# The output product of attention with tokens as the stationary side, and layer norm 2 token block by token block, in an attention-and-mixer kernel

## The chip, the cores and the metric

The kernel runs on one core of a Trainium2 chip. A core has a matrix engine (TensorE, here PE, with PEld for its loads of the stationary operand), VectorE (DVE), ScalarE (ACT), GpSimd (POOL) and SyncE (SP), each with its own instruction stream, and DMA queues between the chip's memory and the on-chip memory. Matmul results go to banks of 128 x 512 floats, from which VectorE and ScalarE read. The metric is the device time of one execution in microseconds (us).

## What is computed

One layer in float32: layer norm, attention in four segments of 512 tokens with a memory carried from one segment to the next, an output product with a residual, a second layer norm, and an MLP with a residual.

```
x = A_x                                      # 1 x 2048 x 1024, 32 heads of 32
o = attention(layernorm(x))                  # 4 segments of 512, causal in each, gated with the memory
h = x + o @ wo                               # wo 1024 x 1024
y = layernorm(h)
h2 = h + gelu(y @ w1 + b1) @ w2 + b2         # w1 1024 x 3584, w2 3584 x 1024
```

## The kernel before

Every product is made of three matmuls, since each operand is split into a high and a low part (`split`, L86): high times high, high times low, low times high (`mm3`, L113). A split is a cast on ScalarE (L90) and a subtraction on VectorE or GpSimd (L91). The moving side of a matmul has 512 columns, the stationary side 128.

The program runs over two halves of 1024 tokens, each of two segments (`sl` 0 and 1) of 512 tokens, and each segment of four token blocks of 128. A half has these stages:

1. attention over groups of four heads (eight groups a segment). Its result `ot` (128 features x 512 tokens) is written to `o_dram`, and `load_o` (L622) reads it back, split into `oh`, `ol`;
2. the output product of segment 0, `wo_seg` (L635), interleaved with the end of attention: 1.3 steps of attention for each of the first 14 steps, then 0.7 (`RA`, `RH`, `RS`). Loads of segment 1's outputs are spread among the steps from step 28 (`PD`) on, every third step (`PS`);
3. the output product of segment 1, again `wo_seg`, interleaved with layer norm 2 of segment 0 (`ln2`, one step of it for two of the product). Here TensorE keeps program order (`in_order(PE)`), the other engines are ordered by the scheduler;
4. `Mixer.lead`: the MLP's first products (`cps`, 24 matmuls per block of features: `c1` and `c2`) on segment 0's tokens, all engines in program order. Beside it, 0.4 side steps per step, run layer norm 2 of segment 1 and `fold`, which transposes the normed tokens and makes the sums and differences of the two segments' tokens that the later products read;
5. 14 times `Mixer.pair`, and in half 1 the second MLP product.

`wo_seg` takes `wo` in eight blocks of 128 columns (`load_block`, L289). A block is the stationary side, the 512 tokens move, so the result `pwo` has features on the partitions. `finish` copies it with ScalarE to `at` (L657); its `fold` transposes `at` in four pieces with TensorE into `pn` (L662), and VectorE adds the four pieces to four token blocks `ht` (L666), which hold `x` at first. A token block has its sum when all eight column blocks are through. `pwo`, `pn` and layer norm's transposes `pt` all turn through the same three banks (`ps_dense`).

Layer norm 2 takes statistics with VectorE (L121, L125) and the scale and offset with GpSimd (L128 to L134, `nb`), norms with ScalarE (L163); `residual` adds `b2` (`hb`, L686) and stores it. `ln_transpose` then turns the block with TensorE (`pt`, L142), casts it on ScalarE (`zh`, L144) and subtracts on VectorE (`zl`, L146). In the lead, the product's first part is copied by ScalarE (`p`, L831) and stored by a DMA that ScalarE issues; the GELU is L779; the weights `wx` are cast on ScalarE (L806) and subtracted on VectorE (L812).

Of the kernel before, what the change touches and what calls it, by code (L numbers as in the profile page):

```python
# [9 lines left out]
F32 = mybir.dt.float32  # L10
# [6 lines left out]
P = 128  # L17
# [8 lines left out]
NG = 8  # L26
HT = 1024
NT = HT // P
RA, RH, RS, PD, PS = 1.3, 14, 0.7, 28, 3
# [13 lines left out]
def build(tc, x, wq, wk, wv, wo, beta, w1, b1, w2, b2, out):  # L43
# [253 lines left out]
    def attention(half, first):  # L297
# [254 lines left out]
        def av_out(st):  # L552
# [82 lines left out]
    def wo_seg(half, sl, hts, tp, extra, evac):  # L635
        blk, wts = {}, {}

        def prods(c, gs):
            for k in (c, c + 1):
                if k < DC and k not in wts:  # L640
                    wts[k] = load_block(wp, wo, k * P, 3, "scalar", "gpsimd" if k % 2 else "vector")
            if c not in blk:
                blk[c] = wts[c] + (ps_dense("pwo"),)
            wh, wl, ps = blk[c]
            oh, ol = acts["o", sl]
            for g in gs:
                mm3(ps, wh[:, g, :], wl[:, g, :], oh[:, g, :], ol[:, g, :], g == 0, g == NG - 1)
                next(extra, None)
                if g == 3:
# [5 lines left out]
        def finish(c):
            at = tp.tile([P, 512], F32, tag="tmp", name="at", bufs=5)
            nc.scalar.copy(at, blk[c][2])  # L657

            def fold():
                pn = ps_dense("pn")  # L660
                for t in range(4):
                    op = nc.tensor.transpose(pn[:, t * P:(t + 1) * P], at[:, t * P:(t + 1) * P], ident)  # L662
                    if t == 0:
                        tc.add_manual_dep(op.ins, acts["mm"].ins.name, NOSYNC, reason="program order")
                for t in range(4):
                    nc.vector.tensor_tensor(hts[t][:, c * P:(c + 1) * P], pn[:, t * P:(t + 1) * P],  # L666
                                            hts[t][:, c * P:(c + 1) * P], op=ALU.add)
            evac.append(fold)

        yield from prods(0, range(NG - 1))  # L670
        yield from prods(1, range(NG - 1))
        if sl == 0:
            load_o(half, sl, NG - 1, tp)
        for c in range(DC):
            yield from prods(c, range(NG - 1, NG) if c < 2 else range(NG))
            finish(c)
# [20 lines left out]
    def ln2_combined(half, hts, zx, pp):  # L697
        for _ in range(3):
            yield
        zh, zl = seg_tiles(1, "z")  # L700
        ts = {n: [zx.tile([P, 4, 512], F32R, tag=f"t{x_}{n}", name=f"t{x_}{n}") for x_ in "hl"] for n in (1, 2, 3)}
# [49 lines left out]
        yield from ln_tiles(lnp, hts, None, None, True, 2, act=True, fold=fold, aside=residual(half, 1, hts, pp))  # L751
# [14 lines left out]
    class Mixer:  # L766
# [22 lines left out]
        def begin(self):  # L789
# [27 lines left out]
            lower(-1)  # L817
            self.early = load, upper, lower, left

        def lead(self):  # L820
# [19 lines left out]
            load(1)  # L840
# [448 lines left out]
```

## Time and profile before

| what | value |
|---|---|
| time, median of 3 runs | 2388.07 us (2385.95 to 2391.18) |
| the profiled execution, its own time | 2383.26 us |
| its span, first to last instruction | 2381.4 us |
| granted TensorE clock, mean | 0.995 |
| segment 0's output product, half 0 and 1 | 71.26 and 69.67 us |
| segment 1's output product | 56.94 and 57.90 us |
| `Mixer.lead` | 88.41 and 88.15 us |

The stage times are from one stage's first matmul to the next stage's, in the profiled execution. A row of the profile names a line of the kernel, an engine, an operation and the tiles, out<-in; in a timeline the number behind `<-` in brackets is the time that the engine stood idle before and what released it. A row of the busy time by stage gives, for each engine, busy us and instructions, then the granted clock (1.00 is full), the DMA engines' busy share and GB/s. A row of the waits gives who waited for whom, us in total, how many times, and the longest.

### The profile page before, as it was taken

How to read it: one execution, taken by the hardware profiler on the slowest of the kernel's cores; microseconds unless marked ns; L12 is line 12 of the kernel's file. 1: busy time of each engine (PE TensorE's matmuls, PEld its weight loads, DVE VectorE, ACT ScalarE, POOL GpSimd, SP SyncE). 2: the span in 40 equal slices, each digit the busy share in tenths (PEclk: the TensorE clock that was granted, in tenths of full speed). 3: DMA queues.
4: the chain of work that ended last, by engine and by line, in shares of the span. 5: the costliest groups of instructions: out<-in, count | busy, mean ns of one | idle time of the engine just before them, and what ended most of it. 6: DMA issues, size and time to landing. Idle time of an engine off the chain costs nothing.

```text
span 2381.4 us, 35726 instructions
## 1 busy us (share of the span) xinstructions
PE 2305.1 (97%) x11873; PEld 1905.9 (80%) x11873; DVE 1571.3 (66%) x3420; ACT 1244.0 (52%) x2587; POOL 1083.3 (45%) x1045
## 2 busy tenths in 40 slices
PE   7999999999999999999999999999999999999999
PEld 5888888877777887888888877787888788888887
DVE  5777777775466555777777776456566676566653
ACT  5676676775364344677777776354334223222321
POOL 4444444444255443455555544235444464246430
PEclk9999999999999999999999999999999999999999
DMA  5333333333466554433333334456557976476762
GB/s 164 98 89 89 83 84 85 89 106 121 144 197 204 181 168 136 124 84 88 84 84 87 81 100 125 148 168 208 164 172 224 347 261 223 154 243 229 251 220 96
DMA packets 348306, 357.49 MB, mean 150 GB/s; under 512 B 26302, under 2 KB 251610, under 8 KB 348122
## 3 DMA queue, kind: packets, MB, share of 16 engines
q1 hardware_dynamic: 284954, 318.50, 44.8%
q10 hardware_dynamic: 63168, 36.71, 5.2%
q8 instruction: 94, 1.54, 0.3%
q14 instruction: 90, 0.74, 0.1%
HBM read 227.64 MB, written 77.14 MB: 128 GB/s over the span
## 4 chain that ended last, share of the span: by engine, by line
PE 72%; DVE 7%; ACT 7%; DMA 4%; POOL 3%; issue 3%; SPq 1%; ACTq 0%; DVEq 0%; POOLq 0%
PE po L1137 21%; PE bps L762 8%; PE dps L762 5%; PE ppt L525 5%; PE po L545 5%; PE pqk L493 3%; PE kps L114 2%; PE kps L116 2%; PE kps L115 2%; PE pwo L114 2%; PE pwo L115 2%; PE pwo L116 2%; PE vps L115 2%; PE vps L114 2%; PE vps L116 2%
## 5 line engine op out<-in xcount | busy, mean ns | idle before, releaser
L509 POOL TENSOR_SCALAR pr<-pr,nm,gate 128x128 f32<-128x128 f32 (+3 forms) x512 | 323.8, 643 | 409.0 <-DVE nm L506 316.3
L502 ACT ACTIVATE pr<-pr,mx 128x256 f32<-128x256 f32 (+3 forms) x512 | 287.8, 563 | 174.8 <-DVE mx L494 170.4
L494 DVE CUSTOM_DVE_ANT_0 pr<-pqk,mask 128x256 f32<-128x256 f32 (+3 forms) x512 | 243.5, 483 | 38.2 <-PE pqk L493 35.5
L532 DVE TENSOR_TENSOR ptl<-ppt,pth 128x512 fp32r<-128x512 f32 (+1 forms) x384 | 227.3, 597 | 59.2 <-ACT pth L527 56.9
L525 PE MATMUL ppt<-ident,pr 128*128 128x128 f32 x1280 | 222.7, 277 | 1.9 <-DVE ptl L532 1.7
L527 ACT CAST pth<-ppt 128x512 fp32r<-128x512 f32 (+1 forms) x384 | 194.2, 518 | 51.3 <-PE ppt L525 46.0
L1147 DVE TENSOR_TENSOR c<-c,po 128x512 f32<-128x512 f32 x160 | 105.3, 683 | 150.4 <-PE po L1137 150.3
L91 POOL TENSOR_TENSOR wl<-wr,wh 128x1024 fp32r<-128x1024 f32 x61 | 145.9, 2392 | 115.1 <-ACT wh L90 57.2
L525 PEld LDWEIGHTS ppt<-ident,pr 128*128 128x128 f32 x1280 | 164.1, 140 | 32.2 <-DVE ptl L532 3.6
L493 PE MATMUL pqk<-ks,qs 96*128 96x256 f32 (+3 forms) x512 | 163.1, 319 | 1.5 <-DVE mx L494 1.5
L545 PE MATMUL po<-ptl,vs 128*64 128x512 f32 (+3 forms) x512 | 154.3, 311 | 5.5 <-DVE ptl L532 5.2
L545 PE MATMUL po<-pth,vs 128*64 128x512 f32 (+3 forms) x512 | 155.7, 326 | 1.3 <-ACT pth L527 1.1
L1137 PE MATMUL po<-w2h,zh 128*128 128x512 f32 x378 | 120.7, 389 | 0.0
L493 PEld LDWEIGHTS pqk<-ks,qs 96*128 96x128 f32 x512 | 96.2, 188 | 26.6 <-DVE mx L494 6.5
L506 DVE RECIPROCAL nm<-mx 128x2 f32<-128x2 f32 x256 | 42.2, 165 | 112.4 <-ACT pr L502 111.9
L1007 POOL TENSOR_TENSOR w2r<-w2r 128x512 f32<-128x512 f32 x54 | 84.3, 1574 | 59.4 <-DMA w2r<-in_B_w 54.6
L114 PE MATMUL kps<-yh,wh 128*128 128x512 f32 x256 | 108.5, 424 | 0.8 <-ACT yh L144 0.8
L114 PE MATMUL vps<-yh,wh 128*128 128x512 f32 x256 | 108.8, 425 | 0.2 <-ACT omt L475 0.2
L114 PE MATMUL qps<-yh,wh 128*128 128x512 f32 x256 | 107.0, 418 | 0.0
L114 PE MATMUL pwo<-oh,wh 128*128 128x512 f32 x256 | 105.7, 415 | 0.7 <-ACT oh L90 0.7
L1137 PE MATMUL po<-w2h,hl 128*128 128x512 f32 x322 | 102.9, 389 | 1.3 <-DVE c L1147 1.3
L116 PE MATMUL pwo<-oh,wl 128*128 128x512 f32 x256 | 102.0, 399 | 0.0
(244 smaller groups left out, 6751.5 us busy)
## 6 DMA issues: line engine op xcount, KB each, us to landing
hr<-h_dram SPq DMA_DIRECT2D x112, 448.0 KB, 4.7
w2r<-in_B_w SPq DMA_DIRECT2D x122, 256.0 KB, 4.4
r<-in_B_w SPq DMA_DIRECT2D x56, 512.0 KB, 4.7
h_dram<-ht ACTq DMA_DIRECT2D x84, 256.0 KB, 3.4
ks<-kh SPq DMA_DIRECT2D x256, 64.0 KB, 2.0
qs<-qh SPq DMA_DIRECT2D x256, 64.0 KB, 2.0
wr<-in_A_wo SPq DMA_DIRECT2D x32, 512.0 KB, 4.4
wx<-in_B_w SPq DMA_DIRECT2D x56, 256.0 KB, 3.8
```

The lines of the kernel that those rows point to most:

```text
L114: nc.tensor.matmul(ps, ah, bh, start=first, stop=False)
L116: acts["mm"] = nc.tensor.matmul(ps, al, bh, start=False, stop=last)
L493: nc.tensor.matmul(pqk[:, :n], u["qs"][j][:, i * P:(i + 1) * P], u["ks"][j][:, 0:n], start=True, stop=True)
L494: nc.vector.tensor_tensor_reduce(out=st["pr"][:, offs[i]:offs[i] + n], in0=pqk[:, :n], in1=mask[:, 512 - n:512], op0=ALU.add, op1=ALU.min, ...
L502: nc.scalar.activation(pi, pi, AF.Exp, bias=mx[:, i:i + 1], scale=-1.0, accum_out=mx[:, 4 + i:5 + i])
L509: nc.gpsimd.tensor_scalar(pi, pi, nm[:, 4 + k:5 + k], gate[:, 1, 4 * g + j:4 * g + j + 1], op0=ALU.mult, op1=ALU.mult)
L525: nc.tensor.transpose(ppt[:, o:o + P], pr[:, offs[i] + jk * P:offs[i] + (jk + 1) * P], ident)
L527: nc.scalar.copy(pth[:, base:base + w], ppt[:, :w])
L532: nc.vector.tensor_tensor(o, x0, x1, op=ALU.subtract)
L545: nc.tensor.matmul(po[:, P * jk:], v, st[part][:, koff[jk]:koff[jk] + w], start=(jk, part) == (0, "pth"), stop=(jk, part) == (2, "ptl"))
L762: nc.tensor.matmul(ps, x_[:, c, :], y_[:, c, :], start=first and c == 0 and n == 0, stop=last and c == 3 and n == 2, skip_group_check=True)
L1137: nc.tensor.matmul(ps, x_[:, k], y_[k], start=opens and k == 0 and i == 0, stop=closes and k == self.KP - 1 and i == 2, skip_group_check=True)
```

## The change

Now 128 tokens of the attention output are the stationary side, and `wo` moves in halves of 512 columns. A result `pwo` has tokens on the partitions and is added to `ht` straight from its bank, by one VectorE instruction (L670 of the changed kernel). The copies `at`, the transposes `pn` and the 128-column adds are gone. The number of product matmuls is the same: two halves `n` by four token blocks `t`, eight groups and three matmuls in each, 192 a segment. `wo` is still loaded in 512 KB pieces, eight a segment, now as 256 rows by 512 columns.

- `wo_first` (segment 0) takes the blocks (n, t) in the order (0,0), (0,1), both without the last group of heads at first, then (0,2), (0,3), (1,0) to (1,3). Two of its weight quarters lie in tiles of a new pool `zt`.
- `wo_second` (segment 1) takes (0,0), (0,1), (1,0), (1,1), (0,2), (1,2), (0,3), (1,3). When both halves of a token block are done, `ready` runs layer norm 2's statistics, residual and norm for it (`ln2_token`). For block 3 they stay in the lead, as do all four `fold`s, which there have no norm between them.
- The last group of attention outputs is split straight from `ot`, without the way through `o_dram`. `PD` is 16 in place of 28. `load(1)` of the mixer's weights is issued in `begin`, within the second product, not at the lead's start.

```diff
-RA, RH, RS, PD, PS = 1.3, 14, 0.7, 28, 3
+RA, RH, RS, PD, PS = 1.3, 14, 0.7, 16, 3
...
-                nc.sync.dma_start(o_dram[u["s"]][u["g"]], ot)
+                if u["g"] < NG - 1:
+                    nc.sync.dma_start(o_dram[u["s"]][u["g"]], ot)
+                else:
+                    oh, ol = o_tiles(half, u["s"] % 2)
+                    split(None, ot, oh[:, NG - 1, :], ol[:, NG - 1, :], hi_eng="scalar", lo_eng="vector")
...
+    def wo_raw(n, k):
+        wr = wp.tile([P, DC, P], F32, tag="wr", name="wr", bufs=2).rearrange("p a b -> p (a b)").rearrange("p (c n) -> p c n", c=2)
+        nc.sync.dma_start(wr, wo[k * 256:(k + 1) * 256, n * 512:(n + 1) * 512].rearrange("(c p) n -> p c n", p=P))
+        return wr
+    def wo_halves(wr, k, home):
+        h, l = home
+        split(None, wr, h, l, "scalar", "gpsimd" if k % 2 else "vector")
+        return h, l
+    def wo_home():
+        return [wp.tile([P, DC, P], F32R, tag=t, name=t, bufs=3).rearrange("p a b -> p (a b)")
+                .rearrange("p (c n) -> p c n", c=2) for t in ("wh", "wl")]
+    def wo_block(half, sl, hts, blk, wts, extra, n, t, gs=range(NG), after=None):
+        if (n, t) not in blk:
+            blk[n, t] = ps_dense("pwo")
+        ps, cols = blk[n, t], slice(t * P, (t + 1) * P)
+        oh, ol = o_tiles(half, sl)
+        for g in gs:
+            wh, wl = wts[n, g // 2]
+            mm3(ps, oh[:, g, cols], ol[:, g, cols], wh[:, g % 2], wl[:, g % 2], g == 0, g == NG - 1)
+            next(extra, None)
+            if after:
+                after(g)
+            if g == NG - 1:
+                o = hts[t][:, n * 512:(n + 1) * 512]
+                nc.vector.tensor_tensor(o, blk.pop((n, t)), o, op=ALU.add)
+            yield
+    def wo_first(half, hts, extra):
+        wts, blk, raws = {}, {}, {}
+        more = [zx_tile(x_, 3) for x_ in "hl"]
+        for k in range(4):
+            wts[0, k] = wo_halves(wo_raw(0, k), k, wo_home() if k < 3 else [x_[:, 0:2] for x_ in more])
+        block = partial(wo_block, half, 0, hts, blk, wts, extra)
+        def turn(g):
+            if g == 0:
+                raws[1] = wo_raw(1, 1)
+            if g % 2 and g < NG - 1:
+                k = g // 2 + 1
+                if k not in raws:
+                    raws[k] = wo_raw(1, k)
+                wts[1, k] = wo_halves(raws[k], k, wo_home())
+        for t in (0, 1):
+            yield from block(0, t, range(NG - 1))
+        for t in (0, 1):
+            yield from block(0, t, range(NG - 1, NG))
+        wts[1, 0] = wo_halves(wo_raw(1, 0), 0, [x_[:, 2:4] for x_ in more])
+        yield from block(0, 2)
+        yield from block(0, 3, after=turn)
+        yield from block(1, 0)
+        acts["raw"] = [wo_raw(0, k) for k in (0, 1)]
+        for t in range(1, 4):
+            yield from block(1, t)
         for _ in extra:
             pass
+    def wo_second(half, hts, ready):
+        wts, blk = {}, {}
+        zxs = {m: [zx_tile(x_, m) for x_ in "hl"] for m in (1, 2, 3)}
+        def weights(n, k):
+            m = 2 * n + k // 2 + 1
+            home = [z[:, 2 * (k % 2):2 * (k % 2) + 2] for z in zxs[m]] if m < 4 else wo_home()
+            wr = acts["raw"][k] if n == 0 and k < 2 else wo_raw(n, k)
+            wts[n, k] = wo_halves(wr, k, home)
+        for k in range(4):
+            weights(0, k)
+        def blocks():
+            block = partial(wo_block, half, 1, hts, blk, wts, iter(()))
+            for n, t in ((0, 0), (0, 1), (1, 0), (1, 1), (0, 2), (1, 2), (0, 3), (1, 3)):
+                for g, _ in enumerate(block(n, t)):
+                    if n == 0 and t < 2 and g % 4 == 1:
+                        weights(1, 2 * t + g // 4)
+                    yield
+                if n == 1:
+                    ready(t)
+        return blocks()
...
-        yield from ln_tiles(lnp, hts, None, None, True, 2, act=True, fold=fold, aside=residual(half, 1, hts, pp))
+        for t in range(4):
+            yield from fold(hts[t], t)
+    def ln2_token(half, hts, pp, t):
+        m, r = ln_scale(lnp, hts[t], True)
+        nb = ln_offset(lnp, m, r)
+        residual(half, 1, hts, pp)(t)
+        yield
+        nc.scalar.activation(hts[t], hts[t], AF.Identity, bias=nb, scale=r)
+        yield
 
...
             lower(-1)
+            load(1)
             self.early = load, upper, lower, left
...
-            load(1)
             for j in (0, 1):
...
+        mixer = Mixer(half, mq)
+        last_token = []
+
+        def ready(t):
+            steps = ln2_token(half, hts1, pp, t)
+            if t < 3:
+                for _ in steps:
+                    pass
+            else:
+                last_token.append(steps)
+
+        second = wo_second(half, hts1, ready)
+        load_x(half, 1, hts1)
         nc.sync.dma_start(acts["b2"], bass.AP(tensor=b2.tensor, offset=b2.offset, ap=[[0, P], [1, D]]))
-        load_x(half, 1, hts1)
-        mixer = Mixer(half, mq)
         with in_order(mybir.EngineType.PE):
-            interleave(hooked(wo_seg(half, 1, hts1, pp, iter(()), evac), lambda k: mixer.begin(), 57, 1),
+            interleave(hooked(second, lambda k: mixer.begin(), 57, 1),
                        ln2(half, 0, hts, pp), 0.5)
         acts.pop("last")
 
         def ln2_last():
             yield
-            yield
-            for e in evac:
-                e()
-            yield from ln2_combined(half, hts1, zx, pp)
+            next(last_token[0])
+            side = ln2_combined(half, hts1)
+            for n, _ in enumerate(side):
+                if n == 1:
+                    next(last_token[0])
+                yield
```

Of the program's instructions 128 go on TensorE (11875 to 11747), 96 on VectorE (3398 to 3302), 32 on ScalarE (2217 to 2185); GpSimd keeps its 1050, SyncE has 1490 in place of 1498.

First, TensorE in half 0, where layer norm 2 of segment 0 begins. Before, `ht_6844` is the first token block, and its transposes stand behind those of the last two column blocks:

```order
L114 MATMUL pwo<-oh_7317,wh 128x512
L115 MATMUL pwo<-ol_7318,wh 128x512
L116 MATMUL pwo<-oh_7317,wl 128x512
L662 MATMUL pn<-ident,at 128x128 [waits Activation_49]
L662 MATMUL pn<-ident,at 128x128 x3
L662 MATMUL pn<-ident,at 128x128 [waits Activation_49]
L662 MATMUL pn<-ident,at 128x128 x3
L142 MATMUL pt<-ident,ht_6844 128x128 [waits DVE_49]
L142 MATMUL pt<-ident,ht_6844 128x128 x3
```

After, the first token block is `ht_6847`, and `zh_7497`, `wh` and their low parts hold quarters of `wo`:

```order
L114 MATMUL pwo<-zh_7497,oh_7177 128x512
L115 MATMUL pwo<-zl_7498,oh_7177 128x512
L116 MATMUL pwo<-zh_7497,ol_7178 128x512
L142 MATMUL pt<-ident,ht_6847 128x128 [waits DVE_49]
L142 MATMUL pt<-ident,ht_6847 128x128 x3
L114 MATMUL pwo<-wh,oh_7177 128x512 [waits Activation_49]
L115 MATMUL pwo<-wl,oh_7177 128x512 [waits DVE_49]
L116 MATMUL pwo<-wh,ol_7178 128x512
```

The transposes of layer norm 2 follow the product directly, and the product's next matmuls wait for casts and subtractions of weights that stand on ScalarE and VectorE.

Second, VectorE in the second output product of half 0. Before (`zl_7624` is layer norm 2 of segment 0, `ht_7560` to `ht_7563` the token blocks of segment 1):

```order
L666 TENSOR_TENSOR ht_7560<-pn,ht_7560 128x128 [waits PE_49]
L666 TENSOR_TENSOR ht_7561<-pn,ht_7561 128x128
L666 TENSOR_TENSOR ht_7562<-pn,ht_7562 128x128
L666 TENSOR_TENSOR ht_7563<-pn,ht_7563 128x128
L146 TENSOR_TENSOR zl_7624<-pt,zh_7623 128x4x128 [waits Activation_49]
L91 TENSOR_TENSOR wl<-wr,wh 128x1024 [waits DMAHW4_49,PE_49,Activation_49]
L146 TENSOR_TENSOR zl_7624<-pt,zh_7623 128x4x128 [waits Activation_49]
```

After (`ht_7488` and `ht_7489` are the first two token blocks of segment 1, `ht_6850` the last of segment 0):

```order
L91 TENSOR_TENSOR wl<-wr,wh 128x1024 [waits DMAHW0_49,Activation_49]
L670 TENSOR_TENSOR ht_7489<-pwo,ht_7489 128x512 [waits PE_49]
L872 TENSOR_TENSOR wl<-wx,wh 128x512 [waits DMAHW3_49,Activation_49]
L121 BN_STATS st<-ht_7489 128x6 [waits DVE_49]
L121 BN_STATS st<-ht_6850 128x6 x2
L146 TENSOR_TENSOR zl_7551<-pt,zh_7550 128x4x128 [waits Activation_49] x2
L670 TENSOR_TENSOR ht_7488<-pwo,ht_7488 128x512 [waits PE_49]
L121 BN_STATS st<-ht_7488 128x6 [waits DVE_49]
L738 TENSOR_TENSOR hb<-ht_7488,b2c 128x1024 [waits DMAHW7_49]
```

One add stands where four were, and statistics of segment 1, the mixer's first weights and the last statistics of segment 0 stand ahead of the first `zl`.

Third, ScalarE in the same stage, after (`L810` is the norm of a token block of segment 1; before, its norms stand in the lead):

```order
L866 CAST wh<-wx 128x512 [waits DMAHW3_49,PE_49]
L144 CAST zh_7550<-pt 128x4x128 [waits PE_49] x2
L810 ACTIVATE ht_7488<-ht_7488,nb,v 128x1024 [waits DMAHW6_49,DVE_49,Pool_49]
L144 CAST zh_7550<-pt 128x4x128 [waits PE_49] x2
L810 ACTIVATE ht_7489<-ht_7489,nb,v 128x1024 [waits DMAHW6_49,DVE_49,Pool_49]
L163 ACTIVATE ht_6850<-ht_6850,nb,v 128x1024 [waits DVE_49,Pool_49]
L144 CAST zh_7550<-pt 128x4x128 [waits PE_49] x4
```

Norms of segment 1's token blocks have moved in between the casts that empty segment 0's `pt` banks.

More of the change, by code (lines that the diff above doesn't have):

```diff
@@ L620, in attention, with o_tiles @@
         return last()
+    def o_tiles(half, sl):
+        if ("o", half, sl) not in acts:
+            acts["o", half, sl] = seg_tiles(sl, "o")
+        return acts["o", half, sl]
     def load_o(half, sl, g, tp):
-        if g == 0:
-            acts["o", sl] = seg_tiles(sl, "o")
-        oh, ol = acts["o", sl]
+        oh, ol = o_tiles(half, sl)
         orr = tp.tile([P, 512], F32, tag="tmp", name="orr", bufs=5)
@@ L633, in load_x @@
             nc.sync.dma_start(hts[t], x[0, r0:r0 + P, :])
[L635 to L649, printed above, removed]
-                    for e in evac:
-                        e()
-                    evac.clear()
-                yield
[L655 to L676, printed above, removed]
@@ new lines, in wo_block @@
+    def wo_block(half, sl, hts, blk, wts, extra, n, t, gs=range(NG), after=None):
+        if (n, t) not in blk:
+            blk[n, t] = ps_dense("pwo")
+        ps, cols = blk[n, t], slice(t * P, (t + 1) * P)
+        oh, ol = o_tiles(half, sl)
+        for g in gs:
[8 more added lines that the diff above has]
+            yield
@@ L695, in ln2, with ln2_combined @@
         yield from ln_tiles(lnp, hts, zh, zl, True, 2, act=True, aside=residual(half, sl, hts, pp))
-    def ln2_combined(half, hts, zx, pp):
-        for _ in range(3):
-            yield
+    def ln2_combined(half, hts):
         zh, zl = seg_tiles(1, "z")
-        ts = {n: [zx.tile([P, 4, 512], F32R, tag=f"t{x_}{n}", name=f"t{x_}{n}") for x_ in "hl"] for n in (1, 2, 3)}
+        ts = {n: [zx_tile(x_, n) for x_ in "hl"] for n in (1, 2, 3)}
         b1h, b1l = acts["z", 0]
@@ L1163, in zx_tile @@
     def zx_tile(x_, n):
-        return acts["zx"].tile([P, 4, 512], F32R, tag=f"t{x_}{n}", name=f"z{x_}{n}")
+        return acts["zt" if n == 3 else "zx"].tile([P, 4, 512], F32R, tag=f"t{x_}{n}", name=f"z{x_}{n}")
     first = opening()
     for half in range(2):
+        acts["zt"] = zt = tc.alloc_tile_pool(name=f"zt{half}", bufs=1, side="right")
         rest = attention(half, None if half else first)
@@ L1179, in pre @@
                     yield
-        def last_o():
-            load_o(half, 1, NG - 1, ab)
-            yield
-        evac = []
-        interleave(wo_seg(half, 0, hts, ab, pre(), evac), chain(rest, last_o()), RA, RH, RS)
+        interleave(wo_first(half, hts, pre()), rest, RA, RH, RS)
         if half == 0:
@@ L1204, in ln2_last @@
             yield
-            yield
-            for e in evac:
-                e()
-            yield from ln2_combined(half, hts1, zx, pp)
+            next(last_token[0])
[4 more added lines that the diff above has]
+                yield
         order = ExitStack()
@@ L1235, in build @@
             zx.release()
+            zt.release()
         else:
@@ L1264, in build @@
         order.close()
-    for p in (cx, cl, lnp, sp, mq, zx, apool):
+    for p in (cx, cl, lnp, sp, mq, zx, zt, apool):
         p.release()
```

## The prediction

> **What bounds the kernel.** I read the page's busy shares and the chain that ended last first, then the busy time by stage, TensorE's waits in the stages that the change touches, and the timeline at the longest wait.
>
> ```profile
> span 2381.4 us, 35726 instructions
> PE 2305.1 (97%) x11873; PEld 1905.9 (80%) x11873; DVE 1571.3 (66%) x3420; ACT 1244.0 (52%) x2587; POOL 1083.3 (45%) x1045
> PE 72%; DVE 7%; ACT 7%; DMA 4%; POOL 3%; issue 3%; SPq 1%; ACTq 0%; DVEq 0%; POOLq 0%
> ```
>
> TensorE is busy for 97% of the span and carries 72% of the chain. So time is saved in two ways only: instructions that TensorE no longer has, and waits of TensorE that end sooner. ScalarE (52%) and GpSimd (45%) count only where TensorE waits for them.
>
> ```profile
> core 0: us, PE busy (x) PEld busy (x) DVE busy (x) ACT busy (x) POOL busy (x), PEclk, DMA share, GB/s
> 520.86:592.12 71.26, 67.32 (x370) 54.68 (x368) 41.58 (x119) 41.12 (x88) 30.65 (x29) 1.00 0.41 125
> 592.12:649.06 56.94, 53.07 (x258) 43.55 (x256) 25.84 (x57) 19.91 (x27) 13.14 (x15) 0.97 0.44 147
> 649.06:737.47 88.41, 81.65 (x373) 66.24 (x372) 53.86 (x60) 50.76 (x74) 45.64 (x36) 1.00 0.66 202
> 1498.14:1556.04 57.90, 54.06 (x257) 44.43 (x256) 25.85 (x57) 19.91 (x27) 13.10 (x15) 0.94 0.42 144
> ```
>
> The first three rows are half 0: the output product of the first segment with the end of attention, that of the second segment, and the mixer's lead. The last row is the second product in half 1. What comes before the output product and after the lead is the old program, instruction for instruction.
>
> ```profile
> PE cps L762 <- ACT p L831: 6.1, 3, 2.9
> PE pt L142 <- DVE ht L666: 3.8, 1, 3.8
> PE pn L662 <- ACT at L657: 1.7, 1, 1.7
> PE cps L762 <- ACT p L831: 4.2, 3, 2.8
> PE pt L142 <- DVE ht L666: 3.7, 1, 3.7
> PE pn L662 <- ACT at L657: 1.9, 1, 1.9
> ```
>
> These are TensorE's longest waits in the three stages, first of half 0, then of half 1. Two kinds hang on the turned result (`at`, `pn`, `ht` L666); the third is the lead's product, whose bank waits for ScalarE's copy `p`.
>
> **Part 1, the transposes go.** Before, each of 32 result blocks is copied out by ScalarE, transposed by TensorE in four pieces and added by VectorE. All of that goes.
>
> ```profile
> 617.01 0.39 PE L114 MATMUL pwo<-oh,wh 128*128 128x512 f32 x1
> ...
> 618.37 0.39 PE L114 MATMUL pwo<-oh,wh 128*128 128x512 f32 x1
> ...
> 618.83 0.39 PE L116 MATMUL pwo<-oh,wl 128*128 128x512 f32 x1
> ...
> 619.06 0.60 PE L662 MATMUL pn<-ident,at 128*128 128x128 f32 x4
> ...
> 619.73 0.40 PE L115 MATMUL pwo<-ol,wh 128*128 128x512 f32 x1
> ```
>
> Six matmuls start between 617.01 and 618.37, so one takes 0.227 us. From 618.83 to 619.73 stand two matmuls and the four transposes: 0.90 − 2 × 0.227 = 0.45 us for four, 0.112 each. There are 128 in the program:
>
> ```profile
> L662 PE MATMUL pn<-ident,at x128: 270/272/328, 552.5 to 1561.8; 128*128 128x128 f32 x128
> ```
>
> 128 × 0.112 = **−14.4 us**, on the engine that is the bound. The products stay: 768 of the same 128x512 matmuls. A check on the stage: the second product has 192 of them and some 64 transposes (its own 32 and layer norm 2's 32), 192 × 0.227 + 64 × 0.112 = 50.8 us against 56.94 and 57.90 measured, so 6.1 and 7.1 us of waits. After, it is 43.6 + 3.6 = 47.2 us of issue.
>
> **Part 2, the waits behind the turned result go.** `pn<-at` is −1.73 − 1.86 = **−3.6 us**, since no product waits for a copy. `pt<-ht` L666 is 3.77 + 3.74: layer norm 2 of the first segment had to wait for the last column block; its transposes now wait for a sum and a norm that were ready blocks ago for token blocks 0 to 2: **−7.5 us**. Behind these two waits comes a slower clock:
>
> ```profile
> 611.02 0.91 PE L142 MATMUL pt<-ident,ht 128*128 128x128 f32 x4 [3.77 <-DVE ht L666]
> ...
> 612.15 0.63 PE L115 MATMUL pwo<-ol,wh 128*128 128x512 f32 x1
> 612.58 0.63 PE L116 MATMUL pwo<-oh,wl 128*128 128x512 f32 x1
> 610.00:620.00 10.00, 8.98 (x39) 7.40 (x40) 5.62 (x15) 5.09 (x6) 1.87 (x1) 0.83 0.65 210
> 1510.00:1520.00 10.00, 6.26 (x28) 5.15 (x27) 6.38 (x12) 5.21 (x7) 3.13 (x3) 0.79 0.68 233
> 1520.00:1530.00 10.00, 10.00 (x47) 8.19 (x46) 2.87 (x7) 4.34 (x7) 2.40 (x1) 0.87 0.38 139
> ```
>
> After the wait the matmuls start 0.43 us apart, and the granted clock of 10 us is 0.83 in half 0, 0.79 and 0.87 in half 1. Lost are 10 × 0.17 = 1.7 and 10 × (0.21 + 0.13) = 3.4, together **−5.1 us** if nothing as long takes the place. The Trainium skill, page "TensorE: Matmul & The Clock Gate", section "HAM oscillation — how this bites in real kernels", says that an idle gap of over about 3.4 us puts the clock back to half speed; the trace agrees at 3.77 and 3.74 us. By that rule a new wait over the same length brings the loss back, which is rival B.
>
> **Part 3, what VectorE and ScalarE do instead.** 32 copies go from ScalarE and 128 small adds from VectorE; 32 adds of 128x512 straight from the product's bank come.
>
> ```profile
> L666 DVE TENSOR_TENSOR ht<-pn,ht x128: 273/280/292, 554.1 to 1562.7; 128x128 f32<-128x128 f32 x128
> L657 ACT COPY at<-pwo x32: 564/587/598, 548.6 to 1556.2; 128x512 f32<-128x512 f32 x32
> L1147 DVE TENSOR_TENSOR c<-c,po 128x512 f32<-128x512 f32 x160 | 105.3, 683 | 150.4 <-PE po L1137 150.3
> ```
>
> The new add isn't in this trace; `c<-c,po` has its shape and a bank as source. 32 × 0.683 = 21.9 against 128 × 0.280 = 35.8 us, and 32 × 0.587 = 18.8 us off ScalarE. None of it is on TensorE's path while three banks turn: a block lasts 24 × 0.227 = 5.44 us and the add 0.68. I cost it at nothing; without that cover it would be 0.68 a block at most, 22 us over the program.
>
> **Part 4, the weights.** As many loads (32 of 512 KB), but a block now needs all four loads of its half, where it needed one.
>
> ```profile
> wr<-in_A_wo SPq DMA_DIRECT2D x32, 512.0 KB, 4.4
> L91 POOL TENSOR_TENSOR wl<-wr,wh 128x1024 fp32r<-128x1024 f32 x61 | 145.9, 2392 | 115.1 <-ACT wh L90 57.2
> L806 ACT CAST wh<-wx 128x1024 fp32r<-128x1024 f32 x13 | 13.6, 1052 | 10.9 <-DMA wx<-in_B_w 5.8 <-ACT ht L779 5.1
> ```
>
> One raw buffer turns in 4.4 + 1.05 + 2.39 = 7.84 us, two of them give a load per 3.9 us, and eight loads take 31 of the second product's 47 us. Fetched ahead (two raw loads are issued before the first product's last three blocks, 16 us) they come in time. In the first product attention's instructions stand between, and I take 1 us for one late quarter per half, **+2 us**; bounds 0 and 3.9 (one load's turn) a half.
>
> **Part 5, new waits in the second product.** Its banks turn through the same three as layer norm 2's `pt`. A block that takes the bank of a `pt` waits for its cast on ScalarE and its subtraction on VectorE, and these are now queued behind the norm of the new token blocks.
>
> ```profile
> L121 DVE BATCH_NORM_STATS2 st<-ht 128x6 f32<-128x512 f32 x8 | 5.1, 678 | 0.0
> L686 DVE TENSOR_TENSOR hb<-ht,b2c 128x1024 f32<-128x1024 f32 x4 | 4.7, 1179 | 0.0
> L163 ACT ACTIVATE ht<-ht,nb,v 128x1024 f32<-128x1024 f32 x4 | 5.0, 1243 | 8.2 <-POOL nb L134 7.8 <-ACT p L831 0.5
> L128 POOL TENSOR_SCALAR v<-mv 128x1 f32<-128x1 f32 x4 | 4.2, 1046 | 33.7 <-DVE mv L125 33.6
> L129 POOL TENSOR_TENSOR v<-v,mhalf 128x1 f32<-128x1 f32 x4 | 3.9, 979 | 0.3
> L134 POOL TENSOR_SCALAR nb<-mv,v 128x1 f32<-128x1 f32 x4 | 2.6, 640 | 0.4
> ```
>
> Two places. On VectorE ahead of the first `zl<-pt` stand the add (0.68), `wl<-wx` (taken as 0.68, for the same 128x512), three statistics (3 × 0.68) and two `zl` of 0.68: 4.8 us, some of it beside the block on TensorE; I take 2.7, a little over half, bounds 0 and 4.8. On ScalarE the norm of the first new token block stands ahead of four casts of `pt`, and itself waits for statistics 0.68, `hb` 1.18, GpSimd 1.05 + 0.98 + 0.64, norm 1.24, cast 0.59 and subtraction 0.68 = 7.04; one block of 5.44 covers it, 1.6 stay, bounds 0 and 3.2 (twice that, for the second block). With 0.4 for later ones: 4.7 a half, **+9.4 us**, bounds 0 and 16.
>
> **Part 6, the lead.** Its own issue is 336 × 0.227 + 36 × 0.112 = 80.3 us, so 8.1 of its 88.41 are waits, mostly 6.1 for `p` L831. ScalarE, in program order, stood 8.2 us before the norms (row L163 above), and `p` behind them. Three of four norms now lie in the second product; GpSimd loses 3 × 2.67 us. Against it, the folds follow each other without a norm between them. The last two of before did so too:
>
> ```profile
> 705.42 1.32 POOL b12t L733
> ...
> 714.51 1.71 POOL b12t L733
> ```
>
> GpSimd began the one 9.1 us after the other. I take 6 us of waits instead of 8 in each half, **−4 us** in all, between −6 and +6 a half.
>
> **The sum**, against the profiled run: −14.4 − 3.6 − 7.5 − 5.1 + 2 + 9.4 − 4 = −23.2, so 2383.26 − 23.2 = 2360.1 us. That run lies 4.8 below the median of 2388.07, so against the median it is **2365 us**, 1.0% faster. A measurement of this kernel can tell about 0.2%, 4.8 us, from no change.
>
> **Rivals.** *A, the lead gives it back.* TensorE's steps ask for a fold about every 7.7 us (my estimate: a side step per 2.5 steps of the lead). At 9.1 each, four in a row fall 5.6 us behind, the casts that wait for GpSimd stand ahead of `p` in ScalarE's order, and the lead's waits rise from 6 to 11.6 a half: +11 us, 2376. For it: the 8.2 us that ScalarE stood still for GpSimd before. Against: the side work also starts its first fold a norm earlier, and ends sooner.
>
> *B, the new bank waits grow as long as those that go (3.7 us).* The first at its upper end, 4.8 in place of 2.7, with the 1.7 or 3.4 of slower clock that the two windows show: (2.1 + 1.7) + (2.1 + 3.4) = 9.3, so 2374. For it: VectorE's long subtraction of weights stands just ahead. Against: a whole block stands between a `pt` and the block that takes its bank.
>
> *C, slower: the weights.* If the second product's first four loads aren't fetched ahead (the raw buffers are held until their split has a home in memory that attention frees), two turns of 7.84 stand open at its start: 15.7 a half. Over both halves 31, so 2365 + 31 = 2396. It decides when the first two raw loads land less than 7.84 us ahead of the stage; slower than before begins at 11.6 a half. Against: 16 us of three blocks stand between.
>
> *D, better:* new waits cost 2 a half and the lead's 2: 2 × 2.7 + 2 × 4 = 13 less, 2352.
>
> *E, it doesn't do what it says:* the transposes only filled time in which TensorE would have waited for the weights or VectorE, so that their 14.4 come back as waits, with B's on top: 2365 + 14.4 + 9.3 = 2389. Against it: VectorE was busy 25.84 of 56.94.
>
> **How the numbers follow.** Forecast 0.54, A 0.15, B 0.12, C 0.05, D 0.07, E 0.07. Faster: forecast, B, D and four fifths of A (the rest is A with other upper bounds on top), 0.85; same: that rest and most of E, 0.09; slower: C and a little of E, 0.06. The range goes from D, 2352, to A with the weights at their upper bound, 2376 + 2 × 2.9 = 2382; C and E are left out.
>
> **What would show it.** Right: no `pn` or `at` row; TensorE's instructions 128 fewer; second products of about 52 us with no wait as long as 3.7 and a clock of 1.00 there; leads of about 86. Wrong: `pwo` waiting for DMA or casts of `wr` (C), for `zl` over 3.7 us with a clock below 0.9 (B), or `cps` waiting over 10 us in all for `p` (A).

## The result and the profile after

| | before | after |
|---|---|---|
| median | 2387.44 us (2385.95 to 2391.18, 4 runs) | 2365.69 us (2361.09 to 2374.35, 4 runs) |
| ratio | 1 | 0.9909, 95% interval 0.9888 to 0.9929 |
| profiled execution, span | 2381.4 us | 2366.6 us |
| first product, half 0 and 1 | 71.3, 69.7 us | 70.9, 67.1 us |
| second product | 56.9, 57.9 us | 48.4, 48.6 us |
| lead | 88.4, 88.2 us | 87.6, 88.9 us |

The change made the kernel 0.91% faster, 21.75 us by the medians; 2365 us had been forecast. The page after, its first lines:

```profile
span 2366.6 us, 35300 instructions
PE 2292.1 (97%) x11745; PEld 1893.0 (80%) x11745; DVE 1583.6 (67%) x3324; ACT 1229.0 (52%) x2555; POOL 1076.3 (45%) x1045
```

TensorE has 128 instructions and 13.0 us of busy time fewer, and is the bound at 97% as before. Busy time by stage after, three stages of half 0, then of half 1:

```profile
521.77:592.65 70.88, 65.62 (x341) 53.19 (x340) 45.68 (x107) 40.19 (x83) 37.97 (x40) 0.98 0.50 162
592.65:641.00 48.35, 47.92 (x226) 39.14 (x224) 27.45 (x37) 18.11 (x21) 9.94 (x15) 1.00 0.38 130
641.00:728.61 87.61, 83.03 (x369) 66.95 (x368) 46.71 (x45) 46.11 (x69) 38.00 (x27) 0.98 0.64 192
1419.99:1487.04 67.05, 62.31 (x329) 50.69 (x328) 47.73 (x102) 38.83 (x80) 39.66 (x40) 1.00 0.49 158
1487.04:1535.67 48.63, 47.88 (x226) 39.14 (x224) 28.63 (x38) 18.73 (x21) 10.69 (x15) 1.00 0.38 133
1535.67:1624.55 88.88, 82.03 (x370) 65.66 (x368) 45.69 (x45) 46.12 (x69) 37.79 (x27) 1.00 0.63 189
```

Against before: first products −0.4 and −2.6, second products −8.6 and −9.3, leads −0.8 and +0.7, together −20.9, where the medians differ by 21.75. (The two profiled spans differ by 14.8 only, mostly because the second MLP product, which the change doesn't touch, took 5 us more in this one: 549.1 us from its first matmul to the end, where the profiled runs of this document go from 543.1 to 551.3.) So the gain is nearly all in the second products. TensorE's waits after, of the first product, the second and the lead in half 0, then of the first and the lead in half 1:

```profile
PE po L545 <- ACT pth L527: 1.6, 1, 1.6
PE po L545 <- DVE ot L556: 1.4, 1, 1.4
...
PE pwo L114 <- DVE zl L146: 0.4, 2, 0.2
...
PE cps L822 <- ACT p L892: 3.8, 3, 2.8
...
PE pm L358 <- DVE om L444: 2.7, 1, 2.7
PE ppt L525 <- DVE ptl L532: 1.3, 1, 1.3
...
PE cps L822 <- ACT p L892: 5.5, 5, 2.8
```

The waits for `at` and for `ht` L666 are gone. In the second product almost none took their place, in the first product waits of attention itself did (`po`, `pm`, `ppt`), and the lead waits for `p` as before. In half 0 the two waits for `po` were followed by a slower clock, 10 us at 0.83 granted, so another 1.7 us:

```profile
541.77:551.77 10.00, 6.97 (x31) 5.29 (x30) 7.30 (x19) 9.34 (x22) 7.06 (x8) 0.83 0.53 178
```

### The profile page after: what moved, and what is told of

It reads as the page before. It is cut to its first block, busy times and chain, and to the rows that moved or that the text cites. A ratio compares the mean times of both kernels' runs of the same rounds, so it can differ in the third digit from the quotient of the medians.

```text
span 2366.6 us, 35300 instructions
## 1 busy us (share of the span) xinstructions
PE 2292.1 (97%) x11745; PEld 1893.0 (80%) x11745; DVE 1583.6 (67%) x3324; ACT 1229.0 (52%) x2555; POOL 1076.3 (45%) x1045
## 4 chain that ended last, share of the span: by engine, by line
PE 73%; DVE 9%; ACT 6%; DMA 5%; POOL 4%; issue 3%; SPq 1%; ACTq 0%; DVEq 0%; POOLq 0%
PE po L1197 20%; PE bps L822 8%; PE dps L822 5%; PE ppt L525 5%; PE po L545 4%; PE cps L822 3%; PE pqk L493 3%; PE kps L114 2%; PE kps L116 2%; PE kps L115 2%; PE vps L114 2%; PE vps L115 2%; PE vps L116 2%; PE qps L114 2%; PE qps L115 2%
## 5 line engine op out<-in xcount | busy, mean ns | idle before, releaser
L91 POOL TENSOR_TENSOR wl<-wr,wh 128x1024 fp32r<-128x1024 f32 x53 | 126.9, 2395 | 90.7 <-ACT wh L90 32.9
L930 POOL TENSOR_TENSOR s<-r 128x512 f32<-128x512 f32 x28 | 42.9, 1531 | 162.0 <-DVE sa L946 102.7
L822 PE MATMUL bps<-zh,sa 128*128 128x512 f32 x336 | 110.8, 391 | 1.6 <-DVE u L960 1.6
L822 PE MATMUL bps<-zh,sb 128*128 128x512 f32 x336 | 111.0, 391 | 0.9 <-DVE u L972 0.9
```

The source lines that it names most:

```text
L822: nc.tensor.matmul(ps, x_[:, c, :], y_[:, c, :], start=first and c == 0 and n == 0, stop=last and c == 3 and n == 2, skip_group_check=True)
```

## The experiments

Stage times are from one stage's first matmul to the next's, half 0 and half 1, in each run's profile; medians are of 4 runs, of 5 for the first and 10 for the sixth. "Pace 0.3" is the edit of the second run. In runs 1 and 12 a product begins with its first transposes.

| kernel | first | second | lead | median us | ratio to before, 95% interval |
|---|---|---|---|---|---|
| before | 71.3, 69.7 | 56.9, 57.9 | 88.4, 88.2 | 2387.44 | 1 |
| changed | 70.9, 67.1 | 48.4, 48.6 | 87.6, 88.9 | 2365.69 | 0.9909 (0.9888 to 0.9929) |
| 1 changed, 128 transposes back | 72.9, 70.7 | 51.1, 51.1 | 88.3, 86.3 | 2372.04 | 0.9950 (0.9930 to 0.9971) |
| 2 pace 0.3 | 69.4, 69.4 | 48.2, 48.1 | 80.0, 80.3 | 2350.97 | 0.9849 (0.9835 to 0.9864) |
| 3 output loads later | 70.4, 68.1 | 48.4, 48.1 | 87.8, 88.0 | 2367.60 | 0.9916 (0.9898 to 0.9933) |
| 4 last group through memory | 67.6, 66.4 | 53.0, 51.6 | 87.4, 87.8 | 2368.40 | 0.9922 (0.9905 to 0.9938) |
| 5 norms back in the lead | 70.6, 69.3 | 48.3, 48.8 | 85.2, 85.1 | 2359.25 | 0.9876 (0.9848 to 0.9904) |
| 6 before at pace 0.35 | 73.3, 69.7 | 58.2, 57.0 | 89.1, 88.7 | 2394.41 | 1.0028 (1.0012 to 1.0044) |
| 7 pace 0.25 | 71.2, 69.6 | 49.2, 48.4 | 80.1, 80.1 | 2350.67 | 0.9844 (0.9818 to 0.9869) |
| 8 pace 0.3, casts on GpSimd | 69.7, 67.5 | 48.2, 48.4 | 80.5, 80.0 | 2350.65 | 0.9845 (0.9818 to 0.9871) |
| 9 pace 0.3, segment 0's group through memory | 67.9, 66.0 | 48.2, 48.4 | 80.3, 80.1 | 2345.42 | 0.9816 (0.9795 to 0.9837) |
| 10 pace 0.3, low parts on VectorE | 67.0, 64.8 | 47.8, 47.8 | 80.1, 80.0 | 2341.96 | 0.9803 (0.9780 to 0.9826) |
| 11 both 9 and 10 | 67.2, 64.7 | 47.8, 47.8 | 80.2, 80.0 | 2336.76 | 0.9794 (0.9780 to 0.9809) |
| 12 as 10, 128 transposes back | 71.7, 69.4 | 51.1, 51.1 | 80.0, 80.0 | 2358.06 | 0.9887 (0.9871 to 0.9904) |

A part of these differences is the slower clock, and it comes and goes with the same code. The first product's code is the same in the changed kernel and in runs 2, 3, 5 and 7. Taken as the stretch's length times what the granted clock lacks to 1.00, the slower clock cost 1.7 us there in half 0 of each but run 2, which had none; in half 1 it cost nothing in the changed kernel, 1.7 us in runs 3 and 5, and 3.4 us in runs 2 and 7. Run 2, half 1:

```profile
1419.20:1429.20 10.00, 8.37 (x35) 7.15 (x36) 7.31 (x20) 5.37 (x14) 4.58 (x6) 0.66 0.52 166
```

Without it this code takes 68.7 to 69.5 us in half 0 and 66.0 to 67.6 in half 1. Runs 1, 4 and 9 to 12 show none of it in their first products, run 8 shows 1.7 us in half 0. So first products are compared below at an equal clock as well.

**What a transpose costs** (1, then 12).

```diff
             blk[n, t] = ps_dense("pwo")
+            for i in range(4):
+                nc.tensor.transpose(blk[n, t][:, i * P:(i + 1) * P], ident, ident)
```

> The changed kernel with four transposes of the identity put ahead of each of the 32 output blocks, into the block's own bank: 128 transposes that nothing reads. Theory (part 1 of the sum: a transpose is 0.112 us of the engine that bounds): the two products of a half grow by 16 x 4 x 0.112 = 7.2 us, the program by 14.4 us against the changed kernel. Rival (E: the transposes only filled time in which TensorE would have waited): the program grows by less than 5 us.

The products grew by 2.0, 2.7, 3.7 and 2.4 = 10.8 us, the median by 6.4; the lead of half 1 was 2.6 us shorter. That is neither theory's number. The 2.0 is too small by the 1.7 us of slower clock that the changed kernel had in half 0 and this run hadn't: at an equal clock both first products grew by 3.7, where 32 × 0.112 is 3.6. In the second products TensorE was busy for the whole 51.05 us, near their issue time with the transposes (47.2 + 3.6): the 1.2 us of waits had been covered. So the last run put the transposes where few waits were left.

> The 0.3 kernel with all low parts of wo on VectorE, and the 128 transposes that nothing reads put back ahead of the output blocks. In the first run they cost 10 us in the four product stages where 14 were expected, and I put the rest down to waits that they covered. Theory: here few waits are left to cover, so 12 to 14.4 us come: first products +3 to 3.6, second products +3 to 3.6 each, 2354 to 2357. Rival (a transpose costs less than 0.112 us beside matmuls): +10 us or less again.

Products +4.7, +3.2, +4.6 and +3.2 = 15.8 us against run 10, the median +16.1. The transposes in that run, then its first and second product in half 0:

```profile
L661 PE MATMUL pwo<-ident x128: 270/272/273, 521.8 to 1530.4; 128*128 128x128 f32 x128
```

```profile
521.84:593.56 71.72, 67.13 (x373) 55.19 (x371) 53.22 (x112) 41.20 (x84) 26.52 (x34) 1.00 0.52 169
593.56:644.61 51.05, 51.05 (x258) 42.45 (x256) 27.28 (x38) 16.96 (x20) 4.55 (x12) 1.00 0.32 111
```

15.8 / 128 = 0.123 us each, 0.10 in the second products alone (3.2 / 32). The first products grew by 1.0 more than 32 transposes at 0.112 each, because other waits came too: TensorE waited 1.7 us for `om` in half 0, where it was 0.2 in run 10, and 0.9 us for `rg` in half 1, where it was nothing. The transposes are paid in full wherever TensorE has no wait to put them in, and the rival of a lower price beside matmuls falls for the sum. The size in the forecast, 14.4, held.

**The lead** (2, 7, 5, 6).

```diff
-            acc += 0.4
+            acc += 0.3
```

> The changed kernel with 0.3 side steps per step of the lead in place of 0.4, so that a fold is asked for every 13.3 steps (about 9.1 us) in place of 10 (6.8 us); GpSimd began folds 9.0 to 9.5 us apart in the changed kernel. Theory A (the casts that wait for GpSimd's sums hold up the copy p on ScalarE): TensorE's waits for p fall from 3.8 and 5.5 us to under 1.5 a half, the slower clock behind the 2.8 us wait goes too, the leads take 82 to 84 us in place of 87.6 and 88.9, and the program gains 8 to 11 us. Rival (the lead waits for its own weights and for DMA): the leads change by less than 1.5 us.

The leads fell from 87.6 and 88.9 to 80.0 and 80.3, by 7.6 and 8.6, and the program by 14.7 us: more than theory A asked. (1.7 of the 7.6 is the slower clock behind the wait of 2.77 us below.) First ScalarE and GpSimd in the changed kernel's lead, around TensorE's longest wait:

```profile
678.01 1.74 POOL L783 TENSOR_TENSOR b12t<-b12t,zh 128x512 f32<-128x512 f32 x1
679.83 1.27 POOL L784 TENSOR_TENSOR b12t<-b12t,zl 128x512 f32<-128x512 f32 x1
681.13 0.62 ACT L775 CAST zh<-b12t 128x512 fp32r<-128x512 f32 x1 [0.17 <-POOL b12t L784]
681.66 0.58 ACT L892 COPY p<-cps 128x512 f32<-128x512 f32 x1
682.29 0.50 PE L822 MATMUL cps<-zh,wh 128*128 128x512 f32 x1 [2.77 <-ACT p L892]
```

GpSimd ends a fold's second difference at 681.1, ScalarE's cast of it stands ahead of `p`, and TensorE has waited 2.77 us when `p` is through. The two leads at pace 0.3:

```profile
638.06:718.07 80.01, 80.01 (x370) 66.15 (x369) 43.72 (x45) 45.97 (x69) 38.00 (x27) 1.00 0.70 210
1526.66:1606.95 80.29, 80.29 (x369) 66.13 (x368) 43.68 (x45) 45.85 (x69) 38.01 (x27) 1.00 0.70 210
```

TensorE is busy for the whole lead. At 0.25 nothing more was to be had:

> The changed kernel with 0.25 side steps per step of the lead. Theory (at 0.3 GpSimd already keeps up, the leads of 80.0 and 80.3 us stand at TensorE's own issue of 79.8): leads 79.8 to 81 us, the program within 2 us of the 0.3 kernel, 2349 to 2353. Rival (ScalarE still falls behind at 0.3 somewhere): another 1 us or more a half. A last fold that comes late could cost: leads of 82 and more.

80.1 and 80.1, the program 2350.67: as the theory said. Then the part of the change that moved the norms:

```diff
-            if t < 3:
-                for _ in steps:
-                    pass
-            else:
-                last_token.append(steps)
+            last_token.append(steps)
```

(and in the lead each block's statistics and norm ahead of its fold, three side steps more per block).

> The changed kernel with layer norm 2 of all four token blocks of segment 1 in the lead, each ahead of its fold, as before (three side steps more per block); the turned product stays. Theory (the block-by-block norm bought little by itself, because the folds that it lets follow each other hold up p as much as the norms did): second products 47 to 48.5 us, leads 87 to 89.5, the program within 3 us of the changed kernel. Rival (moving the norms out of the lead is worth what part 6 gave it, 2 us a half, or more): leads of 90 us and over, the program 4 us or more slower than the changed kernel.

Both were wrong. With the norms back in the lead, the leads take 85.2 and 85.1, 2.4 and 3.8 *less*, and the second products stay at 48.3 and 48.8. Its waits for `p`, first in half 0, then in half 1:

```profile
PE cps L821 <- ACT p L891: 3.1, 3, 1.8
...
PE cps L821 <- ACT p L891: 3.1, 3, 1.8
```

The changed kernel's were 3.8 and 5.5, and in half 0 its slower clock of 1.7 us is gone too. A norm between two folds gave GpSimd time: the folds' differences (L783) begin 9.6 to 18.3 us apart here. Without a norm the folds bunch, 9.0 to 10.6 us apart, and the longest wait is 2.8 in place of 1.8; run 2, without waits, has them 10.5 to 12.9 apart. So at pace 0.4 the block-by-block norm made the lead worse. Run 5's leads are also 3.2 and 3.1 us shorter than those of before; 0.45 of this is four transposes, and what the rest is wasn't tried. What the moved norm did bring is room:

> The kernel before with 0.35 side steps per step of the lead in place of 0.4 (at 0.3 its side work, with four norms between the folds, doesn't end before the lead's last steps need it). Theory (it is the shorter side work of the change that leaves room for a slower pace): the leads of before gain 0 to 4 us each, program 0 to -8 us. Rival (a slower pace gains 8 us a half in any case): leads of 80 to 82 us.

The kernel before got no faster leads at 0.35 (89.1 and 88.7) and was 0.28% slower; 0.3, which freed the changed lead, doesn't fit its longer side work at all. In the kernel before, therefore, the slower pace alone brought nothing at the one value that was tried.

**The first product** (3, 8, 4, 9, 10, 11).

```diff
-RA, RH, RS, PD, PS = 1.3, 14, 0.7, 16, 3
+RA, RH, RS, PD, PS = 1.3, 14, 0.7, 28, 3
```

> The changed kernel with the loads of segment 1's attention outputs begun at step 28 in place of 16. Theory (the earlier loads put casts that wait for a DMA ahead of attention's own copies on ScalarE, 2.5 us of idle time at 541.85): the waits of 1.4 and 1.6 us in half 0 and of 2.7 and 1.3 in half 1 mostly go, the first products take 67 to 69 and 64 to 65 us in place of 70.9 and 67.1, the program gains 4 to 6 us, unless the second product then waits for its outputs. Rival (these waits come from the number of splits beside attention, wherever they stand): under 1.5 us of change in the first products.

It changed nothing, and couldn't tell: the scheduler put these loads where they had been. SyncE's queue in the changed kernel and in this run:

```profile
525.00 10.93 SPq L644 DMA_DIRECT2D wr<-in_A_wo  x4
536.02 1.84 SPq L634 DMA_DIRECT2D orr<-o_dram  x4
```

```profile
524.50 10.87 SPq L644 DMA_DIRECT2D wr<-in_A_wo  x4
535.47 1.86 SPq L634 DMA_DIRECT2D orr<-o_dram  x4
```

Four loads of `wo` hold the queue for 10.9 us, since there are two raw buffers, and the outputs' loads stand behind them. On ScalarE of the changed kernel:

```profile
541.85 0.62 ACT L90 CAST oh<-orr 128x512 fp32r<-128x512 f32 x1 [2.51 <-DMA orr<-o_dram]
542.49 0.57 ACT L550 COPY ot<-po 32x512 f32<-32x512 f32 x1
```

The cast waits 2.51 us for its DMA, attention's copy `ot` is behind it, and TensorE's 1.4 and 1.6 us follow. Taking the casts off ScalarE:

```diff
-        split(None, orr, oh[:, g, :], ol[:, g, :], hi_eng="scalar", lo_eng="vector" if g % 2 else "gpsimd")
+        nc.gpsimd.tensor_copy(oh[:, g, :], orr)
+        nc.vector.tensor_tensor(ol[:, g, :], orr, raw(oh[:, g, :]), op=ALU.subtract)
```

> The changed kernel at 0.3 with the casts of reloaded attention outputs on GpSimd and their subtractions on VectorE, none on ScalarE. Theory (the first product of half 0 waits 1.3 and 1.6 us because ScalarE stands at such a cast until its DMA lands, behind four weight loads in SyncE's queue, ahead of attention's copies): first product of half 0 66.5 to 68 us in place of 69.4; that of half 1, whose waits come from VectorE standing beside GpSimd's subtraction of weights, 68.5 to 70. Rival (ScalarE is late for other reasons): both within 1 us of the 0.3 kernel's 69.4.

These two waits went, but a `pwo` wait for GpSimd (0.9), a `ptl` wait (0.8) and 1.7 us of slower clock came: 69.7 against 69.4, and 68.0 against 69.4 at an equal clock. In half 1, 67.5 is within what equal code shows there (67.1 to 69.6). This is inconclusive for the total. The direct split, undone for both segments:

```diff
-                if u["g"] < NG - 1:
-                    nc.sync.dma_start(o_dram[u["s"]][u["g"]], ot)
-                else:
-                    oh, ol = o_tiles(half, u["s"] % 2)
-                    split(None, ot, oh[:, NG - 1, :], ol[:, NG - 1, :], hi_eng="scalar", lo_eng="vector")
+                nc.sync.dma_start(o_dram[u["s"]][u["g"]], ot)
...
+        load_o(half, 0, NG - 1, acts["ab"])
...
+            load_o(half, 1, NG - 1, ab)
```

(the first in `wo_first`, after seven groups of the first two blocks, the second behind attention).

> The changed kernel with the last group of attention outputs written to memory and read back, as before. Theory: the way through memory costs a write and a read of about 2 to 3 us each beside other work; TensorE waits for the last group at the end of the first two blocks by 0 to 2 us, program 0 to +3 us. Rival (the direct split, one more cast and subtraction in attention's last steps, is what lengthened the first product): the first products get 2 us shorter each.

The program's +2.7 us lies in the theory's band, but not for the theory's reason. The first products got shorter, by 3.3 and 0.7 (1.6 and 0.7 at an equal clock), so the rival was right in half 0 at most, and the second products paid it back, +4.6 and +2.9 (1.7 of the 4.6 is a slower clock behind the first wait below). TensorE's waits there, half 0:

```profile
PE pwo L115 <- POOL wl L91: 1.9, 1, 1.9
PE pwo L115 <- DVE wl L91: 0.8, 1, 0.8
PE pwo L114 <- ACT wh L90: 0.5, 1, 0.5
```

These are weights that come late, rival C's mechanism at a quarter of its price. Undone for segment 0 alone (`if u["g"] < NG - 1 or u["s"] % 2 == 0`, and its `load_o`):

> The changed kernel at 0.3 with segment 0's last group of outputs written to memory and read back as before, and segment 1's split directly. Theory (the direct split of segment 0's group puts casts ahead of attention's own copies on ScalarE and lengthens the first product by 2 to 3 us; that of segment 1's frees attention's memory early, where the second product's weights go): first products 66 to 68 us, second products 48 to 48.5, the program 3 to 5 us under the 0.3 kernel's 2351. Rival (the late weights of the fourth run, second products of 52.9 and 51.6, come from the first product's order, not from segment 1's group): second products of 50 us and over, the program within 2 us of 2351.

67.9 and 66.0, with second products of 48.2 and 48.4, 5.5 us off the program. So the direct split pays in segment 1. In segment 0 it costs about 1 us in half 0 (67.9 against 68.7 to 69.5); in half 1, where run 2 had 3.4 us of slower clock and this run none, no cost is clear, since 66.0 lies within what the same code takes without the slower clock. That it pays by freeing attention's memory for the weights was not tried by itself. The other cause is in half 1 of the changed kernel, on VectorE and GpSimd:

```profile
1428.58 2.35 POOL L91 TENSOR_TENSOR zl<-wr,zh 128x1024 fp32r<-128x1024 f32 x1 [1.44 <-ACT zh L90]
1428.73 2.22 DVE L443 TENSOR_TENSOR rg<-rg,gate 128x8 f32<-128x8 f32 x1
```

The same line over the whole program, ns least, median and most:

```profile
L443 DVE TENSOR_TENSOR rg<-rg,gate x48: 154/168/2224, 85.0 to 1434.7; 128x8 f32<-128x8 f32 x48
```

An operation of 128x8 took 2.22 us beside GpSimd's subtraction of a weight, where its median is 0.168, and `om`, for which TensorE waits 2.7, is behind it.

```diff
-        split(None, wr, h, l, "scalar", "gpsimd" if k % 2 else "vector")
+        split(None, wr, h, l, "scalar", "vector")
```

> The changed kernel at 0.3 with all low parts of wo subtracted on VectorE, none on GpSimd. Theory (in half 1 VectorE took 2.22 us for an operation of 128x8, median 0.168, beside GpSimd's subtraction of 2.35 us, and TensorE waited 2.6 us behind it): that wait goes, the first product of half 1 takes 66.5 to 68 us in place of 69.4; VectorE's 16 more subtractions of 1.2 us stand beside products. Rival (it is VectorE's own queue): the wait stays or moves, 69 us and more, and the second products get longer by 1 us or more.

```profile
522.67:589.66 66.99, 64.24 (x341) 51.86 (x340) 50.66 (x112) 39.65 (x83) 25.50 (x34) 1.00 0.50 175
589.66:637.48 47.82, 47.60 (x225) 39.22 (x224) 27.89 (x39) 18.27 (x21) 5.19 (x13) 1.00 0.37 127
1408.70:1473.50 64.80, 62.70 (x329) 50.61 (x328) 51.24 (x109) 40.31 (x83) 28.06 (x35) 1.00 0.51 173
```

The wait went, with −2.4 and −4.6 us in the first products. Of the 4.6, 3.4 us are the slower clock behind this wait in run 2; against the changed kernel, which had the wait without the slower clock, it is −2.2. VectorE is busier (50.7 in place of 45.1 us there) and TensorE doesn't notice; the longest 128x8 was 0.84 us. The edit also took most of the waits of half 0 (0.6 us for `pth` is left of 1.6 and 1.4): only three loads of `wo`, 8.55 us, stand ahead of the outputs' loads on SyncE, in place of four and 10.93 us, and SyncE no longer waits 4.4 us there for GpSimd's subtraction. ScalarE's cast no longer waited. SyncE in this run:

```profile
525.87 8.55 SPq L644 DMA_DIRECT2D wr<-in_A_wo  x3
534.51 3.14 SPq L634 DMA_DIRECT2D orr<-o_dram  x4
```

Both edits together:

> Both edits of the two runs before together, at 0.3: segment 0's last group through memory, all low parts of wo on VectorE. Theory (both took the same waits out of the first product: attention's engines were late beside the weights' splits): no more than 1 us from each half on top of the better one, 2338 to 2343. Rival (they are different waits and add up): first products of 65 and 63 us, 2334 to 2338.

Its stages equal run 10's (67.2, 64.7): the theory holds for the first products, which is all that the edits touch, and the two took the same waits out. The median, 2336.76, is 5.2 us lower still, under the theory's band and inside the rival's. In the profiles that lies outside the products: the first product starts 3.2 us earlier (519.44 against 522.67), and the second MLP product is 2.9 us shorter (543.1 against 546.0). By their ratios to the kernel before, 0.9794 and 0.9803, the two runs can't be told apart. This is the lowest median, 2.1% under the kernel before (0.9780 to 0.9809).

## Why the prediction was right, step by step

The total was 2365 against 2365.69. That it came so close is luck: by stage the forecast was off by 5 to 8 us, in both directions. Both halves together, us:

| stage | terms | forecast | measured |
|---|---|---|---|
| first product | transposes −6.3, `at` −3.6, late weights +2 | −7.9 | −3.0 |
| second product | transposes −7.2, `ht` −7.5, clock −5.1, new waits +9.4 | −10.4 | −17.9 |
| lead | transposes −0.9, waits −4 | −4.9 | −0.1 |
| sum | | −23.2 | −20.9 |

- **Part 1, right.** 128 transposes were taken at 0.112; run 12 gave 0.123 with the waits that came along and 0.10 in the second products, and run 1 showed that they cost less only where a wait covers them.
- **Part 2, right for the second product.** The waits for `ht` L666 and the slower clock behind them are gone, the granted clock there is 1.00 in place of 0.97 and 0.94. That such a clock could come back elsewhere was not counted: it cost 1.7 us in the first product and 1.7 in the lead of half 0.
- **Part 3, right.** 32 adds of 0.68 to 0.69 cost nothing; no wait of TensorE names them.
- **Part 4, mis-sized and at another place.** Two us of late weights were forecast. Not the product waited for its weights, but attention, 3.0 and 4.0 us in the rows above, behind SyncE's queue and behind VectorE beside GpSimd. I had priced the loads by their turn (7.84 us) and looked only at who waits for weights, not at who stands behind them; the moved splits were not counted on the engines that attention uses. With the low parts on VectorE (run 10) the first products are 67.0 and 64.8, where the forecast's terms give 67.4 and 65.7.
- **Part 5, mis-sized.** 9.4 us of new waits were forecast; 1.2 came by the rows of the waits, 1.9 by the stage's sum. On VectorE the row of work ahead of `zl` ended in time, and TensorE waited 0.18:

```profile
607.14 0.69 DVE L872 TENSOR_TENSOR wl<-wx,wh 128x512 fp32r<-128x512 f32 x1 [2.72 <-ACT wh L866]
607.75 1.87 DVE L121 BATCH_NORM_STATS2 st<-ht 128x6 f32<-128x512 f32 x3
609.53 1.27 DVE L146 TENSOR_TENSOR zl<-pt,zh 128x512 fp32r<-128x512 f32 x2
610.26 0.50 PE L114 MATMUL pwo<-zh,oh 128*128 128x512 f32 x1 [0.18 <-DVE zl L146]
```

  The chain over GpSimd was priced with the lead's rows (1.05, 0.98, 0.64); here, at 613.47 with VectorE idle beside it, the three took 0.19, 0.55 and 0.27, so 1.7 us of the 7.04 weren't there, and the 1.6 that I had left over became 0.24.
- **Part 6, wrong in sign for its reason.** I credited the missing norms with 2 us a half. Run 5 shows that they cost 2.4 and 3.8 at pace 0.4, since the folds bunch; this is rival A's mechanism, at a part of its price. (A's own count was off: ten steps of three matmuls, 6.8 us, lie between two folds, not 7.7.) The rest of the change had made the lead 3 us shorter, so the two nearly cancel. Run 2 shows that at a slower pace nothing else holds the lead.
- **Rivals.** B, the bank waits, didn't come: the longest was 0.5 us. C, the weights, didn't come in the changed kernel, but run 4 brought it about. Of D the first part came, the short new waits, the second, a shorter lead, only with run 2's pace. E, transposes that only filled waits, falls by run 12.

## What to carry to other kernels

A sum over stages should be checked by stage: a right total can stand on terms that cancel, and each of them may be worth more than the change. When side work gets shorter on an engine that copies results in program order, lower its pace: the changed lead went from 87.6 to 80.0 us by one constant. And count the splits of moved loads on every engine beside them, not only for the product that reads them. Read the granted clock beside a stage's time before putting a difference down to an edit: the same first product took 67.1 to 69.6 us in half 1, most of it by the clock.

## What the runs showed of the hardware

- A VectorE operation of 128x8 took 2.22 us while GpSimd subtracted 128x1024 (median 0.168); three small operations of GpSimd took 1.01 us in all with VectorE idle, 2.67 on average in the lead of before.
- The slower clock is not told by the length of one wait. It came behind waits of 1.43 and 1.60 us close together (changed kernel, first product of half 0), of 1.92 us (run 4, second product of half 0) and of 2.63 us (run 2, first product of half 1); it didn't come behind 2.65 us (changed kernel, first product of half 1), 2.98 us (run 4, the same place) and 3.15 us (run 6, lead of half 1).
- The slower clock also followed a wait of 2.77 us. In the lead of half 0 (first row) it came, in that of half 1, after the same wait, it didn't:

```profile
680.00:690.00 10.00, 7.71 (x27) 6.21 (x28) 8.95 (x8) 5.67 (x9) 5.88 (x4) 0.83 0.50 156
1575.00:1585.00 10.00, 6.57 (x28) 4.78 (x27) 8.80 (x8) 6.63 (x11) 7.17 (x5) 1.00 0.49 152
```

  The Trainium skill, page "TensorE: Matmul & The Clock Gate", section "HAM oscillation — how this bites in real kernels", has it after idle gaps of over about 3.4 us; here 2.77 was enough once, and not the other time.
